# Two chained feed-forward layers behind chunked attention: each chunk attends to its own 64 slots, and the weights are normalised on VectorE

## The chip, the core and the metric

The kernel runs on one core of a Trainium2 chip. The metric is the device time of one execution in microseconds (us). The core has five engines that run their own instruction lists in order: TensorE (PE in the profile, with its weight loads as PEld), VectorE (DVE), ScalarE (ACT), GpSimd (POOL) and SyncE (SP, which issues the transfers here).

## What is computed

Attention over chunks of 32 tokens, then two feed-forward layers over all 3072 tokens (4 sequences of 768, 8 heads of 64, model width 512, hidden width 2048), all in 32-bit floats.

```python
chunk, left_ctx, right_ctx = (32, 16, 8)
for c in range(nc):                                   # 24 chunks of each of 4 sequences
    l_start = max(0, c_start - left_ctx)
    r_end = min(S, c_end + right_ctx)
    k_full = np.concatenate([mem_k, k[:, :, l_start:r_end]], axis=2)    # 8 memory slots + 56
    scores = scale * np.matmul(q_c, k_full.transpose(0, 1, 3, 2))
    scores = scores - np.max(scores, axis=-1, keepdims=True)
    a = np.exp(scores)
    a = a / (np.sum(a, axis=-1, keepdims=True) + 1e-09)
    out[:, :, c_start:c_end] = np.matmul(a, v_full)
h = x @ w_in;   g = np.maximum(0.01 * h, h);              x = g @ w_out      # first layer
h = x @ w_in2;  g = h * np.clip(h + 3.0, 0.0, 6.0) / 6.0; x = g @ w_out2     # second layer
```

A chunk in the middle of a sequence has exactly 64 slots: 8 memory slots, 16 tokens to its left, its own 32, and 8 to its right.

## The kernel before

**The feed-forward layers.** Tokens are taken in 6 blocks of 512, the hidden width in 16 slices of 128 (`f`). Per layer, block and slice PE runs 12 matmuls of 128x512 into `ph` (`hidden`) and 12 into `py` (`output`), since each 32-bit operand is split in a high and a low part and three of the four products are kept (`mm3`, L609). That is 4608 matmuls. Between the two, ACT and DVE apply the activation and split it again into `gh` and `gl` (L642, L651). The weights arrive as 64-bit words; converting one slice takes ACT (L219, L225, L253) and DVE (L229, L233, L240, L247, L259) five DVE instructions. The first layer's 32 half-slices are converted at the start and during its block 0, the second layer's during block 5.

**The attention.** Its unit is a pair of neighbouring chunks, 64 tokens: 48 pairs, 8 per block. A pair's 64 queries are multiplied with the 96 slots that the two chunks have together (`a_scores`, L346: 8 matmuls of 64x96, 16 records in the trace). Slots that a chunk may not see are barred, either by a matmul that adds minus infinity first (L337, 13 of the first 16 pairs) or by a mask that DVE adds (`a_masked`, L356). Then DVE takes the maxima (L376, L382), ACT the exponentials and their sums (L422), POOL adds a tiny number to the sums (L433), DVE inverts them (L437), and POOL multiplies the weights `e` by the inverse sums (`a_norm`, L441). The weights are turned, on PE and ACT for the first 16 pairs (`a_turn_pe` L459, `a_turned` L464), on DVE for the others (`a_turn`, L451), and multiplied with the values (`a_values`, L472: 8 matmuls of 64x64, 16 records). ACT and DVE split the result into the parts `xh` and `xl` of the layer's input (L488, L494).

**Where it is done.** The 8 pairs of block 0 come first, before any feed-forward matmul; the gaps on PE there are filled with warm-up matmuls on zeros (`keep_warm`, L701). A later pair is served by a visit: PE leaves the feed-forward matmuls, does the scores of one pair and the values of the pair before, and goes back. From the 17th pair on a visit serves two pairs ("doubled"): scores of two, values of two.

**What sets the order.** The program is written as steps with an engine, a length out of the table `TIME` and a due time. A planner (`Program.order`) runs through them ahead of time, gives each engine the ready step that is due first, fills PE's idle time before the last turning of block 0 with warm-up matmuls, and writes the instructions down in that order. Each engine then keeps it. `BEGIN`, `STEP_FIRST` and the like set due times; `SHIFTED` names pairs whose exponentials ACT takes in one instruction, for more work on DVE.

## Time and profile before

| | |
|---|---|
| device time, median of 3 runs | 1135.75 us (1135.74 to 1136.39) |
| device time of the profiled execution | 1135.49 us |
| its span, first to last instruction | 1133.7 us |
| PE busy | 1124.3 us, 99% of the span |
| PEld busy | 922.2 us, 81% |
| DVE busy | 589.5 us, 52% |
| ACT busy | 464.3 us, 41% |
| POOL busy | 60.9 us, 5% |

The times that follow are those of the profiled execution, counted from its span's start. [...]

### The profile page before, as it was taken

How to read it: one execution, taken by the hardware profiler on the slowest of the kernel's cores; microseconds unless marked ns; L12 is line 12 of the kernel's file. 1: busy time of each engine (PE TensorE's matmuls, PEld its weight loads, DVE VectorE, ACT ScalarE, POOL GpSimd, SP SyncE). 2: the span in 40 equal slices, each digit the busy share in tenths (PEclk: the TensorE clock that was granted, in tenths of full speed). 3: DMA queues.
4: the chain of work that ended last, by engine and by line, in shares of the span. 5: the costliest groups of instructions: out<-in, count | busy, mean ns of one | idle time of the engine just before them, and what ended most of it. 6: DMA issues, size and time to landing. Idle time of an engine off the chain costs nothing.

```text
span 1133.7 us, 16067 instructions
## 1 busy us (share of the span) xinstructions
PE 1124.3 (99%) x6326; PEld 922.2 (81%) x6326; DVE 589.5 (52%) x1280; ACT 464.3 (41%) x1043; POOL 60.9 (5%) x123
## 2 busy tenths in 40 slices
PE   8999999999999999999999999999999999999998
PEld 6787788888888888888888888888888888888887
DVE  6999955465665556656998623223223223222222
ACT  7988733334333343336777423223223223222222
POOL 4111100001000001000000000000000000000000
PEclk9999999999999999999999999999999999999999
DMA  8566421121111112115445102002002001001000
GB/s 261 182 187 188 144 75 38 38 85 65 38 56 57 51 62 75 38 64 184 151 150 178 63 1 75 1 1 75 1 1 75 1 1 38 1 1 38 1 1 37
DMA packets 31660, 78.63 MB, mean 69 GB/s; under 512 B 3424, under 2 KB 3424, under 8 KB 31584
## 3 DMA queue, kind: packets, MB, share of 16 engines
q1 hardware_dynamic: 31584, 77.61, 20.9%
q8 instruction: 49, 0.80, 0.3%
q14 instruction: 27, 0.22, 0.1%
HBM read 65.01 MB, written 12.58 MB: 68 GB/s over the span
## 4 chain that ended last, share of the span: by engine, by line
PE 95%; DVE 3%; ACT 1%; POOL 0%; issue 0%; POOLq 0%
PE ph L609 45%; PE py L609 45%; PE px L472 2%; PE psc L346 1%; DVE wa L240 1%; DVE w L259 0%; DVE wa L229 0%; DVE wa L233 0%; DVE raw L247 0%; ACT e L422 0%; PE warm L701 0%; PE pt L459 0%; DVE mx L376 0%; POOL e L441 0%; PE psc L472 0%
## 5 line engine op out<-in xcount | busy, mean ns | idle before, releaser
L609 PE MATMUL ph<-xh,w 128*128 128x512 f32 x768 | 254.3, 392 | 0.3 <-ACT xh L488 0.2
L609 PE MATMUL ph<-yh,w 128*128 128x512 f32 x768 | 252.0, 389 | 0.0
L609 PE MATMUL py<-gh,w 128*128 128x512 f32 x768 | 239.3, 392 | 0.8 <-DVE w L259 0.8
L609 PE MATMUL py<-w,gh 128*128 128x512 f32 x768 | 236.4, 389 | 0.0
L637 DVE SCALAR_TENSOR_TENSOR ph<-g,ph 128x512 f32<-128x512 f32 x96 | 66.8, 696 | 294.2 <-ACT g L631 294.2
L631 ACT ACTIVATE g<-ph,three 128x512 f32<-128x512 f32 x96 | 66.2, 690 | 299.8 <-PE ph L609 299.8
L609 PEld LDWEIGHTS ph<-xh,w 128*128 128x128 f32 x768 | 143.8, 188 | 31.6 <-DVE w L259 0.7
L609 PEld LDWEIGHTS py<-w,gh 128*128 128x128 f32 x768 | 144.1, 188 | 29.8
L609 PEld LDWEIGHTS ph<-yh,w 128*128 128x128 f32 x768 | 144.0, 188 | 29.9
L609 PEld LDWEIGHTS py<-gh,w 128*128 128x128 f32 x768 | 142.7, 188 | 31.3 <-DVE w L259 1.5
L609 PE MATMUL ph<-xl,w 128*128 128x512 f32 x384 | 149.6, 390 | 0.4 <-DVE xl L494 0.4
L609 PE MATMUL py<-gl,w 128*128 128x512 f32 x384 | 149.6, 390 | 0.0
L609 PE MATMUL py<-w,gl 128*128 128x512 f32 x384 | 149.4, 389 | 0.0
L609 PE MATMUL ph<-yl,w 128*128 128x512 f32 x384 | 149.4, 389 | 0.0
L628 ACT ACTIVATE ph<-ph 128x512 f32<-128x512 f32 x96 | 55.9, 582 | 177.9 <-PE ph L609 177.5
L451 DVE STREAM_TRANSPOSE aT<-e 32x128 f32<-32x128 f32 x384 | 116.0, 302 | 17.5 <-POOL e L441 12.0
L651 DVE TENSOR_TENSOR gl<-ph,gh 128x512 fp32r<-128x512 f32 x96 | 66.3, 690 | 74.1 <-ACT gh L642 73.1
L653 DVE SCALAR_TENSOR_TENSOR gl<-ph,gh 128x512 fp32r<-128x512 f32 x96 | 66.3, 691 | 55.6 <-ACT gh L644 55.6
L609 PEld LDWEIGHTS ph<-xl,w 128*128 128x128 f32 x384 | 72.1, 188 | 15.3 <-DVE xl L494 0.7
L609 PEld LDWEIGHTS py<-gl,w 128*128 128x128 f32 x384 | 72.1, 188 | 15.2
L609 PEld LDWEIGHTS py<-w,gl 128*128 128x128 f32 x384 | 72.1, 188 | 15.2
L609 PEld LDWEIGHTS ph<-yl,w 128*128 128x128 f32 x384 | 72.1, 188 | 15.0
(75 smaller groups left out, 910.0 us busy)
## 6 DMA issues: line engine op xcount, KB each, us to landing
raw<-in_moe_w_in_dram SPq DMA_DIRECT2D x32, 512.0 KB, 3.5
raw<-in_moe_w_out_dram SPq DMA_DIRECT2D x32, 512.0 KB, 3.7
qk_now<-in_qk_dram SPq DMA_DIRECT2D x24, 320.0 KB, 3.8
y_dram<-yo SPq DMA_DIRECT2D x24, 256.0 KB, 2.0
yn<-y_dram SPq DMA_DIRECT2D x6, 1024.0 KB, 6.0
out_dram<-oo SPq DMA_DIRECT2D x24, 256.0 KB, 3.3
in_qk<-in_qk_dram SPq DMA_DIRECT2D x16, 320.0 KB, 4.3
v_now<-in_v_dram SPq DMA_DIRECT2D x24, 192.0 KB, 2.5
```

The costliest lines, as they stand in the source:

```text
L240: nc.vector.scalar_tensor_tensor(out=a, in0=hi, scalar=0xC0000000, in1=a, op0=ALU.bitwise_and, op1=ALU.bitwise_or)
L346: nc.tensor.matmul(pt[j][n * PT:(n + 1) * PT, m * W:(m + 1) * W], qt[r, hp, :], kt[r, hp, :], start=not more, stop=True, tile_position=(e ...
L451: nc.vector.transpose(out=t[c, :, r], in_=e[r, :, c])
L472: nc.tensor.matmul(pt[e * D:(e + 1) * D, at + hp * every:at + hp * every + PT], vt[:, c], t[:, hp, n * PT:(n + 1) * PT], start=True, stop= ...
L609: nc.tensor.matmul(dst, a, b, start=first and i == 0, stop=last and i == len(terms) - 1)
L628: nc.scalar.activation(out=ph, in_=ph, func=AF.Prelu, alpha=0.01)
L631: nc.scalar.activation(out=g, in_=ph, func=AF.Relu, bias=three, scale=1.0)
L637: nc.vector.scalar_tensor_tensor(out=ph, in0=g, scalar=6.0, in1=ph, op0=ALU.min, op1=ALU.mult)
L651: nc.vector.tensor_sub(out=gl, in0=ph, in1=gh.bitcast(F32))
L653: nc.vector.scalar_tensor_tensor(out=gl, in0=ph, scalar=1.0 / 6.0, in1=gh.bitcast(F32), op0=ALU.mult, op1=ALU.subtract)
```

## The change

1. **Slots.** The two chunks of a pair no longer share 96 slots. The host lays out 104 slots for a pair (the 8 memory slots stand at both ends), the first chunk takes the first 64 of them and the second the last 64. Scores are 16 matmuls of 32x64 for a pair in place of 8 of 64x96, each into its own eighth of the array (64 rows by 32 columns). Nothing has to be barred in the middle of a sequence; only the first and last pair of each sequence overwrite a few scores. The barring matmuls, the mask and their memsets go.
2. **What follows from it.** `e` has 256 columns for a pair in place of 384. PE turns it with 2 matmuls in place of 4; DVE with 16 transposes of 32x64 in place of 12 of 32x128. Values are 16 matmuls of 64x32 in place of 8 of 64x64, on four places of 64x64 in place of two of 96x64, and land in two PSUM banks, in the free half of the banks of the visit's scores. So `xh` and `xl` take two instructions each in place of one.
3. **Normalising.** `a_norm` is issued on DVE in place of POOL.
4. **Transfers.** A pair's queries and keys are 344 KB in place of 328, its values 262 KB in place of 197 (128x672 and 128x512 words of 4 bytes, before 128x640 and 96x512).
5. **Order.** `TIME`, `BEGIN`, `STEP_FIRST`, `PAIR_FIRST`, `SHIFTED` (one pair in place of two) and `EARLY` have other numbers, so the planner writes another order. Before the first feed-forward matmul it has 59 pairs of warm-up matmuls (118 records) in place of 46 (92), and the first weights are loaded after the inputs of four pairs in place of one.

```diff
-    visit=1.45, visit2=2.1, scores=0.75, masked=0.56, most=0.55, exp=0.37, exp_all=0.52, small=0.15, inverse=0.18, norm=0.83, turn=0.6, turned=0.57, turn4=0.95,
-    values=0.85, xh=0.4, xl=0.45, half=1.36, act=0.58, six=0.69, gh=0.6, gl=0.69, done=0.66, warm=0.22,
+    visit=1.05, visit2=1.55, scores=0.5, masked=0.5, most=0.42, exp=0.35, exp_all=0.4, small=0.15, inverse=0.18, norm=0.36,
+    turn=0.35, turned=0.38, turn4=0.95, values=0.6, xh=0.52, xl=0.45, half=1.36, act=0.58, six=0.69, gh=0.6, gl=0.69,
+    done=0.66, warm=0.22,
...
-BEGIN = 31.0
-STEP_FIRST, STEP_MIXED, STEP = 7.0, 6.6, 5.5
-PAIR_FIRST = 1.9
-SHIFTED = (3, 5)
-EARLY = 35.0
+BEGIN = 34.0
+STEP_FIRST, STEP_MIXED, STEP = 6.6, 6.6, 5.5
+PAIR_FIRST = 2.1
+SHIFTED = (6,)
+EARLY = 30
...
-        more = barred_by_pe(pr)
-        if more:
-            for j in range(2):
-                nc.tensor.matmul(
-                    pt[j][:, :HP // 2 * W], cls, barred.rearrange("p m w -> p (m w)"),
-                    start=True, stop=False, skip_group_check=True,
-                )
-        for m in range(HP // 2):
-            for j in range(2):
-                hp = j * HP // 2 + m
-                for e in range(2):
-                    r, n = slice(e * D, (e + 1) * D), e ^ j
+        pt = [scores_of(pr, b) for b in range(2)]
+        for h in range(2):
+            for g in range(4):
+                c, n = divmod(g, 2)
+                for b in range(2):
+                    r = slice(b * D, (b + 1) * D)
                     nc.tensor.matmul(
-                        pt[j][n * PT:(n + 1) * PT, m * W:(m + 1) * W], qt[r, hp, :], kt[r, hp, :],
-                        start=not more, stop=True, tile_position=(e * D, n * PT), skip_group_check=more,
+                        pt[b][g * CH:(g + 1) * CH, h, :], qt[r, 2 * c + h, n * CH:(n + 1) * CH],
+                        kt[r, 2 * c + h, n * (W - WIN):n * (W - WIN) + WIN],
+                        start=True, stop=True, tile_position=(b * D, g * CH),
                     )
...
     def a_norm(pr):
-        e, su = e_t[pr], s_t.pop(pr)
-        nc.gpsimd.tensor_tensor(out=e, in0=e, in1=su.unsqueeze(2).to_broadcast([P, HP, W]), op=ALU.mult)
+        e, su = e_t[pr].rearrange("p h b w -> p (h b) w"), s_t.pop(pr)
+        nc.vector.tensor_tensor(out=e, in0=e, in1=su.unsqueeze(2).to_broadcast([P, HP, WIN]), op=ALU.mult)
...
-        for j in range(W // 32):
-            c = slice(32 * j, 32 * j + 32)
-            nc.vector.transpose(out=t[c, :, r], in_=e[r, :, c])
+        for b in range(2):
+            for j in range(WIN // 32):
+                c = b * WIN + 32 * j
+                nc.vector.transpose(out=t[c:c + 32, :, r], in_=e[r, :, b, 32 * j:32 * j + 32])
...
-        for hp in range(HP):
-            nc.tensor.transpose(pt[:W, hp * P:(hp + 1) * P], e[:, hp, :], ident)
+        for h in range(2):
+            nc.tensor.transpose(pt[:, h * P:(h + 1) * P], e[:, h].rearrange("p b w -> p (b w)"), ident)
...
-        for hp in range(HP):
-            for e in range(2):
-                c, n = slice(hp * P + e * D, hp * P + (e + 1) * D), e ^ 2 * hp // HP
-                nc.tensor.matmul(
-                    pt[e * D:(e + 1) * D, at + hp * every:at + hp * every + PT], vt[:, c], t[:, hp, n * PT:(n + 1) * PT],
-                    start=True, stop=True, tile_position=(0, e * D),
-                )
+        for n in range(2):
+            for h in range(2):
+                for b in range(2):
+                    for c in range(2):
+                        o = ((n * 2 + h) * 2 + c) * D
+                        g = 2 * c + n
+                        nc.tensor.matmul(
+                            pt[b][c * D:(c + 1) * D, h, n * CH:(n + 1) * CH], vt[b * WIN:(b + 1) * WIN, o:o + D],
+                            t[b * WIN:(b + 1) * WIN, h, g * CH:(g + 1) * CH],
+                            start=True, stop=True, tile_position=(b * D, c * D),
+                        )
...
-        c = add("POOL", T["norm"], due(4.6), a_norm, pr, after=[c])
+        c = add("DVE", T["norm"], due(4.6), a_norm, pr, after=[c])
```

**A doubled visit on PE**, in block 1. The names: `psc` holds scores, `qk_now` and `in_qk` are two pairs' queries and keys, `aT` turned weights, `v_now` and `in_v` values, `ph` is a feed-forward result. Before, its last scores and all its values:

```order
L346 MATMUL psc_0_2165<-in_qk 64x96 x2
L346 MATMUL psc_1_2166<-in_qk 64x96 x2
L472 MATMUL px_2183<-aT_2068,v_now 64x64 x8
L472 MATMUL px_2183<-aT_2083,in_v 64x64 x8
L609 MATMUL ph_1_7_2158<-xh_758,w_7_1075 128x512
```

Now, its last two scores and the beginning of its values:

```order
L349 MATMUL psc_0_2226<-in_qk 32x64
L349 MATMUL psc_1_2227<-in_qk 32x64
L472 MATMUL psc_0_2226<-aT_2092,v_now 64x32 x2
L472 MATMUL psc_1_2227<-aT_2092,v_now 64x32 x2
```

The visit stands where it stood, between the same kinds of feed-forward matmuls; in it are 32 score matmuls in place of 16 and 32 value matmuls in place of 16.

**DVE at the end of the start**, up to the last `xl` of block 0's eighth pair. `wa`, `raw` and `w` with the numbers of a slice and of its half are steps of the weight conversion (L229, L233, L240, L247, L259 in this order for each half-slice). Before:

```order
L259 TENSOR_TENSOR w_0_438<-raw_0_1_160,w_0_438 128x512
L229 TENSOR_SCALAR wa_2_0_563<-wa_2_0_563 128x512
L233 TENSOR_SCALAR wa_2_0_563<-wa_2_0_563 128x512
L240 SCALAR_TENSOR_TENSOR wa_2_0_563<-raw_2_0_221,wa_2_0_563 128x512
L494 TENSOR_TENSOR xl_286<-px_567,xh_285 128x4x64
L247 ISA raw_2_0_221<-raw_2_0_221,wa_2_0_563 128x512x2
L229 TENSOR_SCALAR wa_1_1_590<-wa_1_1_590 128x512
L233 TENSOR_SCALAR wa_1_1_590<-wa_1_1_590 128x512
L240 SCALAR_TENSOR_TENSOR wa_1_1_590<-raw_1_1_463,wa_1_1_590 128x512
L494 TENSOR_TENSOR xl_286<-px_603,xh_285 128x4x64
```

Now:

```order
L229 TENSOR_SCALAR wa_0_1_663<-wa_0_1_663 128x512
L233 TENSOR_SCALAR wa_0_1_663<-wa_0_1_663 128x512
L259 TENSOR_TENSOR w_1_675<-raw_1_0_188,w_1_675 128x512
L499 TENSOR_TENSOR xl_293<-px_0_678,xh_292 128x2x64
L499 TENSOR_TENSOR xl_293<-px_1_679,xh_292 128x2x64
L240 SCALAR_TENSOR_TENSOR wa_0_1_663<-raw_0_1_239,wa_0_1_663 128x512
L378 TENSOR_REDUCE mx_748<-psc_0_707 128x2
L378 TENSOR_REDUCE mx_748<-psc_1_708 128x2
L247 ISA raw_0_1_239<-raw_0_1_239,wa_0_1_663 128x512x2
L229 TENSOR_SCALAR wa_2_0_726<-wa_2_0_726 128x512
L499 TENSOR_TENSOR xl_293<-px_0_729,xh_292 128x2x64
L499 TENSOR_TENSOR xl_293<-px_1_730,xh_292 128x2x64
```

When the last `xl` is issued, 22 conversion instructions stand ahead of it on DVE before (half-slices 0_0, 1_0, 0_1 whole, 2_0 but for its last, three of 1_1) and 15 now (0_0 and 1_0 whole, 0_1 but for its last, one of 2_0). Up to the conversion's 29th half-slice, the order of both holds the same 29 on DVE, with 16 normalisations among them now.

## Rows read from the trace of the kernel before

**Rows 1.** Page, busy times: us, share of the span, instructions.

```profile
PE 1124.3 (99%) x6326; PEld 922.2 (81%) x6326; DVE 589.5 (52%) x1280; ACT 464.3 (41%) x1043; POOL 60.9 (5%) x123
```

**Rows 2.** Stretches (from:to, length), core 0: each engine's busy us, PEclk, DMA share, GB/s.

```profile
0.00:34.20 34.20, 29.37 (x413) 22.00 (x413) 24.90 (x71) 25.66 (x82) 13.86 (x37) 1.00 0.81 248
34.20:126.02 91.82, 91.00 (x598) 71.64 (x598) 88.22 (x177) 78.91 (x184) 14.06 (x22) 1.00 0.59 185
130.80:505.00 374.20, 374.20 (x2470) 307.92 (x2471) 215.83 (x612) 134.84 (x409) 32.98 (x64) 1.00 0.18 59
```

**Rows 3.** Chain that ended last, whole span: start us, us, engine, tile, line, records.

```profile
141.91 8.16 PE ph L609 x36
...
237.48 8.16 PE ph L609 x36
```

**Rows 4.** Chain that ended last, 140 to 220 us: a doubled visit.

```profile
155.51 0.82 PE psc L346 x32
156.33 1.08 PE px L472 x32
157.41 2.95 PE py L609 x12
160.36 2.72 PE ph L609 x12
```

**Rows 5.** Chain that ended last, 100 to 145 us: a single visit, conversion, turning.

```profile
115.15 0.18 PE psc L337 x2
115.33 0.49 PE psc L346 x16
115.82 0.61 PE psc L472 x16
...
124.75 1.28 DVE w L259
...
127.49 0.44 PE pt L459 x4
```

**Rows 6.** Stretches inside a visit, L346 on PE alone: records under way.

```profile
155.46:155.56 0.10, 0.10 (x4) 1.00 0.00 0
155.58:155.64 0.06, 0.06 (x8) 1.00 0.00 0
155.66:155.72 0.06, 0.06 (x12) 1.00 0.00 0
```

**Rows 7.** Timeline of POOL, 37 to 40 us: start us, us, instruction, idle before it.

```profile
37.86 1.12 POOL L441 TENSOR_TENSOR e<-e,su 128x384 f32<-128x384 f32 x1 [0.36 <-DVE su L437]
```

**Rows 8.** Timeline of DVE, 0 to 60 us.

```profile
31.28 0.42 DVE L494 TENSOR_TENSOR xl<-px,xh 128x256 fp32r<-128x256 f32 x1
31.62 0.68 DVE L247 CUSTOM_DVE_ANT_0 raw<-raw,wa 128x1024 uint16<-128x1024 uint16 x1
...
38.21 1.32 DVE L247 CUSTOM_DVE_ANT_0 raw<-raw,wa 128x1024 uint16<-128x1024 uint16 x1
...
41.68 0.69 DVE L247 CUSTOM_DVE_ANT_0 raw<-raw,wa 128x1024 uint16<-128x1024 uint16 x1
```

**Rows 9.** Groups by line and shape: xcount, busy us, mean ns, idle before.

```profile
L356 DVE SCALAR_TENSOR_TENSOR e<-psc,masks 128x192 f32<-128x192 f32 x70 | 20.5, 349 | 36.3 <-PE psc L346 36.2
L382 DVE TENSOR_REDUCE mx<-e 128x4 f32<-128x384 f32 x35 | 17.8, 543 | 0.0
...
L376 DVE TENSOR_REDUCE mx<-psc 128x2 f32<-128x192 f32 x26 | 8.0, 347 | 0.8 <-PE psc L346 0.8
...
L494 DVE TENSOR_TENSOR xl<-px,xh 128x256 fp32r<-128x256 f32 x9 | 3.7, 407 | 0.0
```

**Rows 10.** Timeline of PE, the start: warm-up, the feed-forward's second matmul.

```profile
13.21 1.04 PE L701 MATMUL warm<-idle 128*128 128x256 bf16 x8
...
34.21 0.50 PE L609 MATMUL ph<-xl,w 128*128 128x512 f32 x1 [0.38 <-DVE xl L494]
```

More of the change, by code (lines that the diff above doesn't have):

```diff
@@ L487, in a_xh @@
         c = slice((i - 1) * PT if doubled(pr) else i * PT, (i + 1) * PT)
-        nc.scalar.copy(out=x_t[0, blk][0][:, :, c], in_=px_t[pr])
+        for b in range(2):
+            nc.scalar.copy(out=x_t[0, blk][0][:, 2 * b:2 * b + 2, c], in_=px_t[pr][b])
     def a_xl(pr):
@@ L557, in attention @@
         if direct:
-            c = add("DVE", T["most"] + 0.06, due(1.2), a_most, pr, after=[c])
+            c = add("DVE", T["most"], due(1.2), a_most, pr, after=[c])
             c = add("POOL", T["small"], due(1.8), a_scaled, pr, after=[c])
             if pr in SHIFTED:
-                c = add("DVE", T["masked"] + 0.06, due(2.0), a_shift, pr, after=[c], takes=e, frees=s)
+                c = add("DVE", T["masked"], due(2.0), a_shift, pr, after=[c], takes=e, frees=s)
                 c = add("ACT", T["exp_all"], due(2.6), a_exp_all, pr, after=[c])
@@ L568, in attention @@
         else:
-            c = add("DVE", T["masked"] + 0.06, due(1.1), a_masked, pr, after=[c] + set_up, takes=e, frees=s)
+            c = add("DVE", T["masked"], due(1.1), a_edge, pr, after=[c] + set_up, takes=e, frees=s)
             c = add("DVE", T["most"], due(1.7), a_most, pr, after=[c])
@@ L587, in attention @@
         if blk == 0:
[L588 removed]
+            p = [("ph", ("v", pr, b)) for b in range(2)]
             c = add("PE", T["values"], due(7.0), a_values_first, pr, after=[c, vl], takes=p, frees=aT + vv)
@@ L597, in visit_step @@
             return add("PE", T["scores"], t, visit, pr, after=[*after, opened[-1]], takes=takes, frees=frees)
-        p = [("ph", ("x", pr))] if doubled(pr) else takes[-1:]
+        p = takes or [(f"pa{j}", ("s", pr, j)) for j in range(2)]
         c = add("PE", T["visit2"] if doubled(pr) else T["visit"], t, visit, pr,
-                after=[x for q in pending for x in q[:2]] + [*after], takes=[*takes] + (p if doubled(pr) else []),
+                after=[x for q in pending for x in q[:2]] + [*after], takes=p,
                 frees=[k for q in pending for k in q[2]] + [*frees])
```

185 lines of the change are left out of this document (86 added, 99 removed).

## The prediction

> **What bounds the kernel now.** I read the page first: PE is busy for 1124.3 of 1133.7 us [rows 1], and the stretch 130.8 to 505 us has no idle on it [rows 2]. So from there on an instruction off PE costs nothing unless PE comes to wait for it, and a microsecond taken from PE's list is a microsecond of the end. Next, the chain of waits: in block 1 it is PE alone. Twelve feed-forward matmuls take 2.72 us. A doubled visit is 0.82 us of scores and 1.08 us of values, and the twelve matmuls behind it take 2.95, that is 0.23 more [rows 4]: **2.13 us a visit**. The check is the distance of two blocks, 237.48 - 141.91 = 95.57 us [rows 3]: 32 times 2.72 are 87.04, and four visits at 2.13 are 8.52.
>
> The time ahead of that has two parts. Until 34.2 us PE is busy 29.4 us, much of it warm-up, and the feed-forward starts when the last of block 0's attention is there: its second matmul waits for `xl` [rows 2, 10]. From 34.2 to 126 us PE is full, but so nearly is DVE, 88.2 of 91.8 us, ACT less with 78.9 [rows 2]: weights are converted just ahead of their use, and at 124.75 the chain leaves PE for a conversion's last step [rows 5]. PE and DVE bound that part together. DVE has 24.9 + 88.2 = 113.1 us of work up to 126 us and 12.9 us idle, 9.3 of them in the start.
>
> **The doubled visits.** The order holds 16 visits with scores of two pairs, 15 with values of two, one with values of one, and one last with values alone: 32 pairs' scores and 33 pairs' values. First the old price in parts. A record of the turning takes 0.44 / 4 = 110 ns for 128 columns [rows 5], 0.86 ns a column, one at a time. A score record of 96 columns would take 82 ns alone. They follow each other by 0.82 / 32 = 25.6 ns, so 3.2 run beside each other on the four places they use. The stretches show how: between 155.46 and 155.56 four are under way and none starts, then eight, then twelve [rows 6]; they start in groups of four, a group each 82 ns. A value record of 64 columns would take 55 ns, and they follow by 1.08 / 32 = 33.8: 1.6 on two places. Both come to 80% of the places.
>
> Now there are 64 score records of 64 columns, 55 ns alone, on eight places. At 80% of eight, 6.4, they follow by 8.6 ns: 64 of them take 0.55 us. If no more than 3.2 run at a time, which is the most a row shows, they take 1.10. I take 0.55, since the share of places was the same on two and on four. The 64 value records have 32 columns, 27.5 ns alone, on four places: at 3.2 they follow by 8.6 ns, again 0.55 us. But each still loads weights of 64 columns, and no row shows a place taking such weights more often than each 55 ns; at that pace 64 x 55 / 3.2 = 1.10 us, as now. Between 0.55 and 1.10 no row is nearer, so I take 0.8. With 0.23 for leaving and coming back a visit is 1.58 us. That is 16 x 0.27 for scores and 16.5 x 0.28 for values: **8.9 us less**. The bounds are 1.33 us a visit (13 less) and 2.43 us (4.9 more).
>
> [...] No row here shows a 64-column load under a shorter matmul.
>
> **What DVE pays for the normalising.** 48 of them move from POOL; 16 lie before 126 us. A DVE instruction over 256 columns has a mean of 407 ns, and the next starts 0.34 us after it (31.28 to 31.62) [rows 8, 9]: I take 0.38, 16 x 0.38 = 6.1 us more. Against it stands what POOL's multiplication does to DVE now. At 37.86 it runs on POOL for 1.12 us; the DVE instruction issued at 38.21 takes 1.32 us, where the same one takes 0.69 at 41.68 [rows 7, 8]. This stands at all eight multiplications between 34.2 and 126 us, up to the 1.28 us at 124.75 [rows 5], with 0.5 to 0.6 us more each, 4.6 together; in the start I count 1.1. With POOL's instruction gone these go: 5.7 less.
>
> The other DVE instructions up to there, by the difference of 192 and 384 columns, 347 and 543 ns [rows 9], some 1 ns a column: 26 maxima of 128 for 192 columns, -1.8; ten mask and shift instructions of 192 become eight of 128, two at 20.5 / 70 = 0.29 and eight by 0.07, -1.1; five reductions of 384 become four of 256, one at 17.8 / 35 = 0.51 and four by 0.13, -1.0; 15 `xl` become 30 halves, 15 more starts at 0.07 (the 0.34 us less 256 columns at 1 ns), +1.0. The sum is 6.1 - 5.7 - 1.8 - 1.1 - 1.0 + 1.0 = **2.5 us less work on DVE**, to the same 29th half-slice. After 130.8 us DVE has 216 of 374 us of work [rows 2]; 32 normalisations there add 12 and are hidden, as are 16 transposes of half the columns in place of 12.
>
> **The start.** PE's list there gains 26 warm-up records at 1.04 / 8 = 0.13 us [rows 10], +3.4. It loses eight barrings of 0.18, -1.4; half of eight turnings of 0.44, -1.8; and on nine pairs' scores of 0.49 and eight pairs' values of 0.61 [rows 5], at the ratios above (0.55 of 0.82, 0.8 of 1.08), -1.5 and -1.3. That is 2.6 less, and the feed-forward starts at 31.6 if PE's waits stay as they are. If scores and values gain nothing there, 34.4; if the waits shrink with the chain's shorter steps, 29. The transfers don't stop it: queries and keys of the eighth pair have the same 5.4 MB up to and with them, as weights now stand behind more of the inputs. The later weights are what the start pays with: 7 conversion instructions fewer are done when the feed-forward starts, 3.9 us by the conversion's five steps of some 0.35 to 0.69 us. DVE's work in the start is then 24.9 - 3.9 - 0.7 (mask memsets), the other changes there cancelling within 0.5: 20.3 us. Idle is 31.6 - 20.3 = 11.3 in place of 9.3.
>
> So up to the 29th half-slice DVE has 2.5 + 0.7 = 3.2 us less work and 2.0 us more idle: 1.2 us earlier. PE would be through sooner (it saves visits and turnings here too), so what it saves in block 0 is not counted. Behind 34.2 us DVE had 3.6 us idle while PE was as full as itself; with PE waiting for DVE some of it goes, from none to half. I take a quarter, 0.9: **2.1 us earlier**. The bounds: a start of 34.4 us has 14.1 idle, 4.8 more, and gives 1.6 later; a start of 29 has 0.6 less, and with half of the 3.6 gives 5.6 earlier.
>
> **The sum.** 8.9 + 2.1 = 11.0 us off a device time of 1135.49 us for the profiled execution (span 1133.7, 1.8 us around it) is 1124.5. The median of the runs is 0.26 us above that execution: 1124.7.
>
> **Rivals.** (a) Slower: small matmuls have a floor. The shortest mean distance of records is 25.6 ns, that of the scores. If that is what an instruction costs PE and not the sharing of places, 128 records take 3.28 us a visit: +0.82 on scores and +0.56 on values, 16 x 0.82 + 16.5 x 0.56 = 22.4 us more, 1158 with the start as it was. It turns against the change from 1.90 us / 128 = 14.8 ns a record. Against it: records start in fours with a pause of a record's length between [rows 6], so four are issued in less than a third of that length, and the pause follows the columns.
> [...]
> (b) Slower: neither eight places nor shorter value records help, 2.43 us a visit: +4.9, -2.1 in block 0, 1138.5. Nothing in the trace runs on eight places, so nothing excludes it.
> (c) Faster by less: one of the two helps and the other doesn't (1.88 us a visit, 4.1 less), or DVE holds block 0 up (1.6 later in place of 2.1 earlier): 1128.5 to 1133.
> (d) Faster by more: both at their best, 13 off in the visits, and 5.6 off in block 0: 1117.
>
> **How the numbers follow.** Forecast, 1120 to 1128.5: 0.57. (c), 1128.5 to 1133: 0.17. (d), under 1120: 0.11, a third of that under 1116. (b): 0.07, and (a): 0.08. The range 1116 to 1133 leaves out (a), (b) and the tail of (d), 0.19. A measurement of this kernel can tell about 0.2% from no change, 2.3 us. Faster by more: 0.57 + 0.17 + 0.11 = 0.85. Of (b), between its cases, 0.03 lies within 2.3 us and 0.04 above: same 0.03, slower 0.12.
>
> **What would show it.** In the changed profile a doubled visit's scores should be one piece of the chain of 64 records in 0.5 to 0.6 us, its values 64 records in 0.55 to 1.1, and two blocks 93 to 94 us apart. DVE instructions of 1.0 to 1.3 us in block 0 should be gone, with the normalisation near 0.4 us. The first feed-forward matmul should come at 29 to 34 us, and between it and 125 us PE should wait for conversions where it is full now. I am wrong if the visit comes to 2 us or more, if `gl` comes late behind normalisations and transposes so that PE waits in blocks 1 to 4, or if block 0 ends later than now.

## The result, and the profile after

The changed kernel takes **1142.53 us** (median of 4 runs, 1141.01 to 1144.28) against 1135.74 for the kernel before beside it: a ratio of 1.0057 [1.0045, 1.0069], slower by 0.57% where 0.97% faster (1124.7 us) was forecast. The profiled execution took 1143.07 us, its span is 1141.3 us, 7.6 us above that of before.

Busy times of the changed kernel, as in [rows 1]: PE's hardly moved, though it has 1504 records more.

```profile
PE 1124.9 (99%) x7830; PEld 920.2 (81%) x7830; DVE 590.1 (52%) x1453; ACT 455.6 (40%) x1082; POOL 26.4 (2%) x94
```

The same three stretches as in [rows 2] (from:to, length, then the engines' busy us with records, PEclk, DMA share, GB/s), changed kernel:

```profile
0.00:34.20 34.20, 29.15 (x678) 21.51 (x678) 19.32 (x68) 20.95 (x90) 4.71 (x21) 0.95 0.64 232
34.20:126.02 91.82, 87.13 (x787) 67.32 (x783) 86.51 (x191) 75.12 (x183) 6.43 (x13) 0.98 0.58 197
130.80:505.00 374.20, 372.14 (x3508) 305.26 (x3508) 216.92 (x744) 130.56 (x427) 13.96 (x59) 1.00 0.21 68
```

In the start DVE does 19.3 us of work where it did 24.9. From 34.2 to 126 us PE, which was as good as full (0.8 us idle), is idle for 4.7 us, and behind 130.8 us, where it had no idle at all, it has 2.1. Of the 4.7 us the larger part is put down to ACT, to the step L253 of the weight conversion: four waits of 0.7 to 0.8 us. The page of the changed kernel, then of before, first group of feed-forward matmuls (whole run; behind the last bar the idle time ahead, and what ended most of it):

```profile
L616 PE MATMUL ph<-xh,w 128*128 128x512 f32 x768 | 259.3, 396 | 7.5 <-ACT w L253 3.1
```

```profile
L609 PE MATMUL ph<-xh,w 128*128 128x512 f32 x768 | 254.3, 392 | 0.3 <-ACT xh L488 0.2
```

So DVE isn't the only engine that PE waits for in block 0. No run alters ACT's order alone.

Where the 7.6 us arise is read best from the feed-forward matmuls, which are the same 4608 in both kernels. This table is worked out from their starts in the traces: the start before, and by how much each kernel is later (+) at the same matmul, when both are counted from their first matmul of all (at 1.04 us of the span, at 1.17 in the kernels with the wider warm-up of `w_512`). The second matmul stands at the opening of block 0, and 349 near its end; 433 lies in block 1; at 769, 1153 and 1537 the blocks 2, 3 and 4 begin.

```
matmul  before   after n_pool b_norm b_turns s_early s_old  w_512   c_1    c_3    c_5
     2   34.21   +1.91  +1.27  -1.04   +1.27   +4.26  +2.77  -1.06  +1.74  +1.95  +2.48
    97   59.85   +2.53  +1.86  -1.05   +2.82   +3.29  +3.25  -0.61  +0.77  +1.11  +2.84
   349  130.69   +4.90  +3.16  +0.42   +5.29   +3.74  +3.40  +1.79  +1.27  -0.83  +1.04
   433  149.90   +5.22  +3.59  +0.42   +7.22   +4.07  +5.95  +2.12  +3.19  +1.09  +2.96
   769  234.59   +5.09  +3.45  +0.42   +5.14   +3.94  +3.73  +1.99  +1.08  -1.02  +0.85
   865  258.49   +5.99  +4.19  +0.70   +5.13   +4.84  +4.61  +2.89  +1.06  -1.03  +0.81
  1153  330.17   +5.89  +4.09  +0.70   +5.03   +4.74  +4.51  +2.79  +0.94  -1.15  +0.69
  1249  354.06   +6.83  +4.99  +0.99   +5.39   +5.69  +5.47  +3.94  +1.31  -0.75  +0.65
  1537  425.74   +6.73  +4.88  +0.99   +5.29   +5.59  +5.37  +3.84  +1.19  -0.87  +0.53
  1633  449.63   +7.68  +5.78  +1.27   +5.65   +6.54  +6.33  +5.60  +1.58  -0.51  +0.52
  4608 1129.55   +7.60  +5.70  +1.27   +5.57   +6.46  +6.26  +5.52  +1.48  -0.60  +0.43
```

For the changed kernel that is +4.9 in the start and block 0, +0.3 at the beginning of block 1 (not followed up), +2.8 in three steps of 0.9 where blocks 2, 3 and 4 begin, and -0.4 over the visits, which were to give 8.9. The visit, the block's end and the start each have their own cause. (In row 433 a jump of some 2 us that is gone in row 769, as in `b_turns`, says only that one visit stands ahead of that matmul there and behind it before.)

**The visit.** Timeline of PE, changed kernel, the visit that answers to [rows 4] (start us, us, instruction; a group's us run from its first start to its last end; the ends of matmuls are modelled by the profile, so paces are read from starts):

```profile
160.65 0.46 PE L349 MATMUL psc<-qk_now 64*32 64x64 f32 x32
160.92 0.59 PE L349 MATMUL psc<-in_qk 64*32 64x64 f32 x32
161.44 0.67 PE L472 MATMUL psc<-aT,v_now 64*64 64x32 f32 x32
161.93 0.65 PE L472 MATMUL psc<-aT,in_v 64*64 64x32 f32 x32
```

From the first score to the first value it is 0.79 us (before 0.82), from there to the matmul at 162.50 it is 1.06 (before 1.08), and by the starts around it the way out and back costs 0.25 (before 0.23): 2.10 us in place of 2.13, the same in nearly all visits. The last record of a group of scores lasts 0.216 us, so the first 32 start within 0.46 - 0.22 = 0.24 us, 7.7 ns apart. The second 32 start within 0.59 - 0.22 = 0.37 us, 12 ns apart. Then nothing starts for 0.15 us, and the values follow by (0.67 - 0.22) / 31 = 14.6 ns, on four places, so that a place takes one each 58 ns.

**A block's end.** Timeline of DVE, changed kernel, where block 1 ends, then PE's of the same time (in brackets the idle time ahead and what ended it):

```profile
241.56 0.69 DVE L658 TENSOR_TENSOR gl<-ph,gh 128x512 fp32r<-128x512 f32 x1
242.17 0.68 DVE L689 COPY yo<-py 128x512 f32<-128x512 f32 x1
242.88 4.98 DVE L447 STREAM_TRANSPOSE aT<-e 32x64 f32<-32x64 f32 x20
247.89 0.69 DVE L658 TENSOR_TENSOR gl<-ph,gh 128x512 fp32r<-128x512 f32 x1
```

```profile
248.64 0.50 PE L616 MATMUL ph<-xh,w 128*128 128x512 f32 x1 [0.64 <-DVE gl L658]
```

Between two `gl` stand a copy and 20 transposes in one piece, so the second `gl` comes 247.89 - 241.56 = 6.33 us behind the first. PE needs 2 x 2.72 = 5.44 us for the two groups of twelve matmuls that it runs meanwhile, 0.89 less, and it waits: the next matmul into `ph` is released by that `gl`. The 0.89 us are the step in the table. Before, with 12 transposes there, the two `gl` stood 5.11 us apart, and PE didn't wait:

```profile
236.66 0.69 DVE L651 TENSOR_TENSOR gl<-ph,gh 128x512 fp32r<-128x512 f32 x1
237.26 0.68 DVE L682 COPY yo<-py 128x512 f32<-128x512 f32 x1
237.98 3.77 DVE L451 STREAM_TRANSPOSE aT<-e 32x128 f32<-32x128 f32 x12
241.77 0.69 DVE L651 TENSOR_TENSOR gl<-ph,gh 128x512 fp32r<-128x512 f32 x1
```

**The start.** Timeline of PE, changed kernel:

```profile
17.41 0.41 PE L349 MATMUL psc<-in 64*32 64x64 f32 x21
20.12 0.45 PE L349 MATMUL psc<-in 64*32 64x64 f32 x11 [2.30 <-issue]
20.51 2.85 PE L708 MATMUL warm<-idle 128*128 128x256 bf16 x14
```

In the middle of one pair's scores PE stops for 2.30 us, and nothing that the profile shows ("issue") ended it. Behind it 14 warm-up matmuls take 2.85 us, 0.20 us each where it was 1.04 / 8 = 0.13 before [rows 10]. The stretches show the clock, and how full the transfers were:

```profile
15.00:18.00 3.00, 2.82 (x97) 1.86 (x94) 2.29 (x7) 2.33 (x12) 0.33 (x1) 1.00 1.05 393
18.00:21.00 3.00, 0.88 (x14) 0.58 (x15) 0.37 (x2) 0.69 (x4) 0.23 (x1) 0.75 1.00 393
21.00:24.00 3.00, 3.00 (x66) 2.09 (x65) 1.77 (x7) 1.29 (x8) 0.52 (x1) 0.68 0.16 57
36.00:39.00 3.00, 3.00 (x9) 2.40 (x9) 2.68 (x7) 3.00 (x11) 0.23 (x1) 0.59 0.65 217
```

The granted clock is 1.00 until 19.49 us, 1.67 us after PE came to stand, then 0.50 until 22.90 us, and DVE and ACT have next to nothing to do from 18 to 21 us. It is 0.50 a second time from 36.56 to 39.96 us, behind PE's wait of 1.48 us for `xl` ahead of the first feed-forward matmul (36 to 39 us: 0.59). That a stop brings the clock down isn't shown: in `n_pool` the clock is 1.00 from 18 to 30 us, around a stop of 2.54 us. The kernel before had no stop for "issue" in its start, and its clock stands at 1.00 in all these stretches. Up to the end of the 29th half-slice, one stretch of each kernel (changed, then before; DVE is the third engine):

```profile
0.00:131.43 131.43, 120.90 (x1479) 91.95 (x1479) 110.86 (x269) 100.86 (x287) 12.46 (x35) 0.97 0.59 204
```

```profile
0.00:126.01 126.01, 120.37 (x1011) 93.64 (x1011) 113.11 (x247) 104.56 (x266) 27.91 (x59) 1.00 0.65 202
```

DVE's work fell by 2.3 us, its idle time rose from 12.9 to 20.6.

### The profile page after: what moved, and what is told of

It is laid out like the page before. It is cut to its first block, busy times and chain, and to the rows that moved or that the text cites. A ratio compares the mean times of both kernels' runs of the same rounds, so it can differ in the third digit from the quotient of the medians.

```text
span 1141.3 us, 19214 instructions
## 1 busy us (share of the span) xinstructions
PE 1124.9 (99%) x7830; PEld 920.2 (81%) x7830; DVE 590.1 (52%) x1453; ACT 455.6 (40%) x1082; POOL 26.4 (2%) x94
## 4 chain that ended last, share of the span: by engine, by line
PE 87%; DVE 7%; ACT 3%; issue 1%; POOL 0%; ACTq 0%; POOLq 0%; DVEq 0%
PE py L616 41%; PE ph L616 41%; DVE aT L447 2%; PE psc L472 2%; PE psc L349 1%; ACT e L416 1%; PE warm L708 1%; DVE wa L240 1%; DVE w L259 1%; DVE raw L247 1%; DVE gl L658 1%; ACT w L253 0%; ACT gh L649 0%; ACT wa L219 0%; DVE wa L233 0%
## 5 line engine op out<-in xcount | busy, mean ns | idle before, releaser
L616 PE MATMUL ph<-xh,w 128*128 128x512 f32 x768 | 259.3, 396 | 7.5 <-ACT w L253 3.1
L447 DVE STREAM_TRANSPOSE aT<-e 32x64 f32<-32x64 f32 x512 | 120.9, 236 | 7.4
```

Of the source, the lines that this page charges most:

```text
L447: nc.vector.transpose(out=t[c:c + 32, :, r], in_=e[r, :, b, 32 * j:32 * j + 32])
L616: nc.tensor.matmul(dst, a, b, start=first and i == 0, stop=last and i == len(terms) - 1)
```

## The experiments

Each kernel differs from the changed one by the diff shown ("..." marks what is left out of it), but for `b_norm`, which starts from the kernel before. The changed kernel took 1142.53 us; the kernel before, beside the others, 1135.9 to 1136.1 us.

### Which half of the change costs the time

`n_pool`: chunks keep their own slots, POOL multiplies.

```diff
-        nc.vector.tensor_tensor(out=e, in0=e, in1=su.unsqueeze(2).to_broadcast([P, HP, WIN]), op=ALU.mult)
+        nc.gpsimd.tensor_tensor(out=e, in0=e, in1=su.unsqueeze(2).to_broadcast([P, HP, WIN]), op=ALU.mult)
...
-        c = add("DVE", T["norm"], due(4.6), a_norm, pr, after=[c])
+        c = add("POOL", T["norm"] + 0.3, due(4.6), a_norm, pr, after=[c])
```

> The changed kernel with the multiplication by the inverse sums back on POOL (planned with 0.66 us there); chunks keep their own 64 slots. Theory: the engine of this step is not what costs the time. Block 0 loses 16 times 0.43 us of DVE and gets holds of DVE by POOL back, of 0.3 to 0.6 us each: within 1.5 us of 1142.5. Rival: normalising on VectorE lengthens what stands ahead of `gl` and of the conversions and is the cause of the loss: 1136 to 1139 us.

Measured: 1141.94 us, ratio to before 1.0054 [1.0037, 1.0071]. The theory holds: with slots of their own, the engine of this step isn't what costs the time. DVE is through with the 29th half-slice at 129.69 us, 1.7 us sooner than in the changed kernel:

```profile
0.00:129.69 129.69, 121.21 (x1489) 92.18 (x1489) 107.32 (x254) 100.08 (x287) 21.84 (x51) 0.99 0.61 207
```

That is 3.5 us less work than with the multiplication on DVE, holds included, and 1.8 us more idle. The 0.6 us between the medians is inside the scatter of the runs.

`b_norm`: the same two lines in the kernel before, the other way round (`nc.vector`, `"DVE"`, `T["norm"] - 0.3`).

> The kernel before with the other half of the change alone: the weights are multiplied by their inverse sums on VectorE (planned with 0.53 us), 96 slots for a pair as before. Theory: the move costs and gives about the same in block 0 (16 times 0.53 us of DVE for 384 columns, 8.5 us, against holds of 5.7 us) and is hidden later: 1136 to 1139 us. Rival: it is the half of the change that costs the time: 1141 us or more.

Measured: 1138.79 us (1136.75 to 1140.34), ratio 1.0023 [1.0014, 1.0033]. So this half alone costs 2.8 us, inside the expected range, and the other half alone (`n_pool`) 5.9; together 6.8. Of the 2.8 the profiled execution, the shortest of its ten, shows 0.4 in block 0 and three steps of 0.28 at the block ends. In it DVE is through with the 29th half-slice at 126.43 us, 0.4 us later than before:

```profile
0.00:126.43 126.43, 120.50 (x1017) 94.26 (x1017) 116.05 (x263) 103.48 (x265) 10.93 (x43) 1.00 0.64 201
```

That is 2.9 us more work on DVE and 2.5 us less idle, and PE, which waits for that step in both kernels, is later by the same 0.4 us.

### The visit

`v_swap`: the scores of the second pair first.

```diff
-            a_scores(pr)
             if doubled(pr):
                 a_scores(pr + 1)
+            a_scores(pr)
...
```

(Left out: whichever pair comes first now takes the two banks.)

> The changed kernel with the two pairs' scores of a doubled visit in the other order: the 32 records on `in_qk` first, then the 32 on `qk_now`. In the changed kernel the first 32 (on `qk_now`) start within 0.24 us, the second 32 take 0.38 us and more. Theory: PE holds only so many instructions ready, and those beyond arrive at a slower pace; so whichever pair stands second is the slow one, here `qk_now`. Rival: the operand `in_qk`, which lies in a buffer of the raw weights, is what is slow: then the first 32 are spread now, and the second 32 start within 0.24 us. The time is that of the changed kernel, 1142.5 us, by both.

Measured: 1140.92 us, one run. Timeline of PE:

```profile
181.05 0.45 PE L349 MATMUL psc<-in_qk 64*32 64x64 f32 x32
181.31 0.59 PE L349 MATMUL psc<-qk_now 64*32 64x64 f32 x32
```

The second 32 are the slow ones again, now those on `qk_now`: it isn't the operand `in_qk` that is slow.

`v_32`: values with 32 weight columns, first halves ahead of second halves, in doubled visits.

```diff
-                            start=True, stop=True, tile_position=(b * D, c * D),
...
+        k = 32 if doubled(pr) else D
+        for d in range(0, D, k):
...
+                            r = c * D + d
...
+                                start=True, stop=True, tile_position=(b * D, r),
```

> The changed kernel with each value matmul of a doubled visit cut in two of 32 weight columns, all first halves ahead of all second halves: 128 records in place of 64, each on a place of 64x32, on four places at a time. In the changed kernel a place takes a value record each 58 ns, with 32 columns moving as with the 64 of before. Theory: it is the load of 64 weight columns that takes those 58 ns. Then 32 columns take about half, 128 records follow by some 7.3 ns, values take 0.93 us in place of 1.06 and a visit 1.95 in place of 2.08: 2 us less in 16 visits, 1140.5 us. Rival: a place takes 58 ns for a record whatever its columns: 128 records take 1.86 us, a visit 2.9 us, 1155 us.

Measured: 1149.96 us, ratio 1.0120 [1.0105, 1.0136]. The time misses both, yet the visit answers the question. Timeline of PE, an undisturbed visit, its larger groups:

```profile
211.30 0.54 PE L349 MATMUL psc<-in_qk 64*32 64x64 f32 x28
211.61 0.21 PE L475 MATMUL psc<-aT,v_now 64*32 64x32 f32 x1
...
211.68 0.71 PE L475 MATMUL psc<-aT,v_now 64*32 64x32 f32 x60
...
212.22 0.75 PE L475 MATMUL psc<-aT,in_v 64*32 64x32 f32 x62
```

60 records start within 0.71 - 0.19 = 0.52 us, 8.8 ns apart; on four places that is one each 35 ns, where 64 weight columns took 58. So a place isn't held 58 ns whatever its columns; that it is the load of the weights which takes them, and not what else hangs on their number, is the likely reading. Two more things are seen. Values start at 211.61, before the last scores have started: the pause of 0.15 us between scores and values is gone here, where both use places of 64x32. And behind the first 32 scores the records come by some 9 ns on the mean, scores or values, so the 35 ns may be that pace and the load shorter. With twice the records at this pace the undisturbed visit still takes 2.10 us, where the theory had 1.95. The 7.4 us lost against the changed kernel lie elsewhere. With 192 records a visit PE stops inside visits, too:

```profile
162.98 0.60 PE L475 MATMUL psc<-aT,in_v 64*32 64x32 f32 x44
165.53 0.37 PE L475 MATMUL psc<-aT,in_v 64*32 64x32 f32 x18 [1.95 <-issue]
```

and the waits at the block ends grew with it.

`v_first`: values ahead of both pairs' scores. The function `visit` in short:

```diff
-        a_scores(pr); a_scores(pr + 1)
         for i, p in enumerate(of):
             a_values(p, [x[:, :, i * PT:(i + 1) * PT] for x in px])
+        a_scores(pr); a_scores(pr + 1)
```

> The changed kernel with the values of a visit ahead of its scores; nothing else differs, the planner's list is the same. Theory: behind the first 32 records PE's instructions come by some 8.3 ns a record (with the values in 128 records, they followed by 16.6 ns for two), so the second 32 score records were spread. A place takes a value record each 58 ns, four places one in 14.6 ns, slower than instructions come, so some are ready again when the scores begin. Expected: 64 values in 1.0 us, then 64 scores without the spread, 0.5 to 0.6 in place of 0.79 us, a visit of 1.85 to 1.95 in place of 2.08 us, 2 to 3 us less in 16 visits: 1139.5 to 1140.5 us. Rival: the second pair's scores are slow for being the second 32 on the same places: a visit stays at 2.08 us and the time at 1142.5 us.

Measured: 1142.55 us (1140.70 to 1145.60). The visit is what it was, 1.06 and 0.79 us, with 32 scores starting within 0.24 and 32 within 0.38 us again. The expected gain wasn't there. That left two readings: more than 32 records without a pause, or the second use of the same places.

`v_mid`: values between the two pairs' scores, edited likewise.

> The changed kernel with the values of a visit between the scores of its two pairs. The second 32 score records were spread whichever pair they belong to and whatever stands ahead of the first 32. Theory: some 32 records are ready ahead of PE, later ones come by 8.3 ns; the values take 14.6 ns a record, so 32 are ready again behind them. Expected: both pairs' scores start within 0.24 us each; one more change between scores and values costs 0.15 us, so a visit stays near 2.08 us. Rival: the second use of the same places is what is slow: the second pair's records are spread over 0.37 us again, and a visit takes 2.2 us. Time 1141 to 1145 us by both.

Measured: 1141.28 us, one run. Timeline of PE:

```profile
181.41 0.45 PE L347 MATMUL psc<-qk_now 64*32 64x64 f32 x32
181.79 0.67 PE L470 MATMUL psc<-aT,v_now 64*64 64x32 f32 x32
182.28 0.65 PE L470 MATMUL psc<-aT,in_v 64*64 64x32 f32 x32
182.85 0.46 PE L347 MATMUL psc<-in_qk 64*32 64x64 f32 x32
```

Both pairs' scores go within 0.24 us now, on the same places. So it is the second 32 of 64 in a row that are slow (0.37 us), and not the second use of the places (0.24); the visit is no shorter (2.08 us), as the 0.14 us gained pay one more pause of 0.15.

### The start

`w_512`: each pair of warm-up matmuls in one (the zeros have 512 columns).

```diff
-    idle = at.tile([P, 256], BF, tag="idle", name="idle")
+    idle = at.tile([P, 512], BF, tag="idle", name="idle")
...
-        for c in range(2):
-            r = slice(c * 256, c * 256 + 256)
-            nc.tensor.matmul(late["warm"][:, r], idle[:, :P], idle, start=True, stop=True)
+        nc.tensor.matmul(late["warm"], idle[:, :P], idle, start=True, stop=True)
```

> The changed kernel with each pair of warm-up matmuls of 256 columns written as one of 512: the same time on PE by the columns, 59 instructions with their 59 weight loads less in the start. In the changed kernel PE stops for 2.30 us at 17.82 us, in the middle of a pair's scores, after 347 of its records; in other variants of it PE stopped 2.2 to 2.5 us at the 221st or the 347th record, at whatever place of the program that was, and each time 2.4 to 2.6 us behind the start of a 16 KB transfer of PE's own instructions. Theory: PE runs out of instructions, as their transfer stands behind the inputs' transfers. Expected: with 31 records less up to that place the stop goes or moves to another place of the program, again at about the 221st or 347th record; if it goes, the 2.30 us and the slow clock behind it (1.2 us) are off the start, and the time is 1139 to 1140 us. Rival: PE waits there for a pair's inputs: it stops in the same scores as before, 1142.5 us.

Measured: **1140.28 us** (1138.87 to 1141.19), ratio 1.0037 [1.0024, 1.0049], 2.2 us less than the changed kernel. The stop stands one pair's scores later in the program, with 20 of 32 still to come, and lasts 0.86 us in place of 2.30:

```profile
19.21 0.33 PE L349 MATMUL psc<-in 64*32 64x64 f32 x12
20.40 0.41 PE L349 MATMUL psc<-in 64*32 64x64 f32 x20 [0.86 <-issue]
```

The stretches up to the long stop, of the changed kernel, `v_first`, `n_pool`, `s_old` and `w_512`, point to the cause; the first number in brackets is PE's records until then.

```profile
0.00:20.10 20.10, 15.58 (x347) 10.85 (x347) 7.79 (x30) 11.15 (x53) 2.83 (x15) 0.98 0.93 340
```

```profile
0.00:19.10 19.10, 15.44 (x347) 10.70 (x347) 7.74 (x30) 11.17 (x53) 2.85 (x15) 1.00 0.93 340
```

```profile
0.00:19.65 19.65, 15.08 (x346) 10.80 (x347) 6.12 (x26) 11.01 (x52) 5.00 (x18) 1.00 0.93 337
```

```profile
0.00:21.60 21.60, 16.10 (x346) 11.54 (x347) 10.77 (x39) 12.13 (x50) 3.17 (x14) 1.00 0.91 337
```

```profile
0.00:20.35 20.35, 17.28 (x346) 8.10 (x346) 9.81 (x37) 12.53 (x61) 3.35 (x16) 1.00 0.92 338
```

In all five PE stands after 346 or 347 records, at different places of the program (the first two have the same start). The stop ahead of it stands after 220 or 221: 0.54 us in the changed kernel, 1.83 in `s_old`, 2.38 in `s_early`. Between the two lie 126 matmuls with as many weight loads. In the changed kernel a 16 KB transfer of instructions starts 2.52 and 2.60 us ahead of the two stops' ends (at 11.43 and 17.52 us), and the transfers ran at 378 and 397 GB/s meanwhile. The reading: PE has used up what it holds before the next 16 KB are there. Its rival, that PE waits there for a pair's inputs, doesn't fit a stop that moves through the program with the count of records. That these transfers are PE's follows from their number in the whole run, 61 for 15660 matmuls and loads and 49 before for 12652, one for each 257 or 258; between the two stops lie 252 of them. The queue of these transfers in the first 34.2 us (number, MB, share of 16 engines), changed kernel, then before:

```profile
q8 instruction: 5, 0.08, 0.9%
```

```profile
q8 instruction: 3, 0.05, 0.6%
```

The kernel before had used 286 records up to 23.1 us, the changed one 347 before 18.

`s_early`: weights' transfers earlier (`EARLY` 38 in place of 30).

> The changed kernel with `EARLY` at 38 in place of 30: the first weights are loaded behind the inputs of one pair, as before the change, and 21 conversion instructions stand ahead of the start's last `xl` on DVE in place of 15. Theory: DVE's idle of the start, some 8 us more than before the change, comes from the weights' late transfers and is what block 0 ends later by. Expected: six instructions of about 0.6 us done earlier, so 3 to 4 us less idle on DVE up to the first feed-forward matmul, that matmul still at about 35.8 us, block 0's last conversion 3 to 4 us earlier, 1139 us. Rival: the transfers are full in the start, so inputs of later pairs come later by the weights put ahead of them (three times 0.5 MB at some 390 GB/s, 4 us): the first feed-forward matmul moves to 38 to 40 us, and the time stays at 1142.5 us or grows.

Measured: 1141.44 us (1139.73 to 1141.92), ratio 1.0044 [1.0029, 1.0059]. Both happen. The first feed-forward matmul is 2.3 us later than in the changed kernel, as the rival had it, with the stop at the 221st record 2.38 us long; and with six conversion instructions more behind it, block 0 ends 1.2 us earlier in the profiled execution. The 1.1 us between the medians lies within the overlap of the runs.

`s_old`: the planner's dates of before.

```diff
-BEGIN = 34.0
-STEP_FIRST, STEP_MIXED, STEP = 6.6, 6.6, 5.5
-PAIR_FIRST = 2.1
-SHIFTED = (6,)
-EARLY = 30
+BEGIN = 31.0
+STEP_FIRST, STEP_MIXED, STEP = 7.0, 6.6, 5.5
+PAIR_FIRST = 1.9
+SHIFTED = (3, 5)
+EARLY = 35.0
...
-            attention(pr, block_at[0, blk] - (6 if blk == 1 else 6) - every * (NPB - i), blk == 1, 1.6 if blk == 1 else 3.4)
+            attention(pr, block_at[0, blk] - (4.5 if blk == 1 else 6) - every * (NPB - i), blk == 1, 1.6 if blk == 1 else 3.4)
```

> The changed kernel with the planner's dates of before: `BEGIN` 31, `STEP_FIRST` 7.0, `PAIR_FIRST` 1.9, `SHIFTED` (3, 5), `EARLY` 35 and 4.5 for block 1's pairs; 18 conversion instructions stand ahead of the start's last `xl` in place of 15. Theory: the start's loss comes from PE (warm-up written between the pairs, and the stop for instructions), so the dates alone give back little: 1140 to 1143 us. Rival: the new dates are what costs DVE its idle: block 0 ends where it did before the change, some 5 us earlier, 1137 us.

Measured: 1141.98 us (1139.70 to 1142.49), ratio 1.0049 [1.0034, 1.0064]: the theory's. It has the stops of 1.83 and 1.60 us, and the dates alone aren't the cause (1.5 of the 4.9 us at matmul 349 in the table).

### The block ends

`b_turns`:

```diff
-    turn=0.35, turned=0.38, turn4=0.95, values=0.6, ...
+    turn=0.35, turned=0.38, turn4=1.1, values=0.6, ...
```

> The changed kernel with one number of the planner's table altered: four transposes of DVE are planned with 1.1 us in place of 0.95. The planner then writes 16 of them between two `gl` at the end of blocks 1 to 4 where it wrote 20. Theory: 20 transposes and a `gl` take 4.98 + 0.69 = 5.67 us, PE needs 5.44 us for the two groups of twelve matmuls that run meanwhile, and it waits for the second `gl`; that is the 0.9 us by which each of these blocks is longer than before. Expected: the 0.9 us goes at the four block ends, 3.6 us together, 1139 in place of 1142.5 us. Rival: the transposes written behind the second `gl` make the visit's values late instead and PE waits there: no change, 1142.5 us.

Measured: **1140.47 us** (1137.15 to 1141.10), ratio 1.0032 [1.0021, 1.0043], 2.1 us less than the changed kernel. DVE at the end of block 1:

```profile
242.93 3.97 DVE L447 STREAM_TRANSPOSE aT<-e 32x64 f32<-32x64 f32 x16
246.94 0.69 DVE L658 TENSOR_TENSOR gl<-ph,gh 128x512 fp32r<-128x512 f32 x1
```

The second `gl` now comes 5.33 us behind the first, in place of 6.33, and PE doesn't wait. (The expectation got its 0.9 us from 5.67 against 5.44, which is 0.23; it left out the copy between the two `gl`.) In the table the step at block 2 is gone, those at blocks 3 and 4 are 0.36 in place of 0.95: 2.1 of the 2.8 us. (The expectation counted four ends; three have the step.)

### Together

`c_1` is `w_512`, `b_turns` and `s_early` in one.

> The changed kernel with the three edits together that each took some time off: warm-up in matmuls of 512 columns, the planned 1.1 us for four transposes, and `EARLY` at 38. Theory: the three act at different places (the stop of PE in the start, the block ends, the conversions ahead of the first feed-forward matmul), so their gains add: -2.2, -2.1 and -1.1, 1137 us, still above the kernel before. Rival: the earlier weights bring the stop for instructions back, as the transfers stand longer: 1139 to 1141 us.

Measured: 1137.05 us (1136.71 to 1138.55), ratio 1.0009 [1.0000, 1.0019]: the gains add, as expected (5.5 us of 6.8), and 1.1 us above the kernel before are left. `c_3` has the values ahead of scores as well, and this:

```diff
-        nc.vector.tensor_tensor(out=e, in0=e, in1=su.unsqueeze(2).to_broadcast([P, HP, WIN]), op=ALU.mult)
+        (nc.gpsimd if pr < 2 * NPB else nc.vector).tensor_tensor(out=e, in0=e, in1=su.unsqueeze(2).to_broadcast([P, HP, WIN]), op=ALU.mult)
...
-        c = add("DVE", T["norm"], due(4.6), a_norm, pr, after=[c])
+        c = add("POOL" if pr < 2 * NPB else "DVE", T["norm"] + 0.3 * (pr < 2 * NPB), due(4.6), a_norm, pr, after=[c])
```

> All of these together: warm-up of 512 columns, 1.1 us planned for four transposes, `EARLY` at 38, values ahead of scores in a visit, and the multiplication by the inverse sums on POOL for the first 16 pairs and on VectorE for the rest. Theory: 1137 by the first three, 2 to 3 us less by the visits, and 1 to 2 less as DVE's list of block 0 gets shorter (3.5 us less work up to the 29th half-slice with POOL multiplying, 2 us more idle): 1132 to 1134 us, less than either kernel. Rival: in block 0 the chain over POOL is longer and PE waits for it, and the visits' gain is not there: 1137 us or more.

Measured: 1134.90 us (1134.50 to 1137.22), ratio 0.9992 [0.9983, 1.0002]. Block 0 came out as expected, 2.1 us below `c_1`; the visits gave nothing, so it misses the expected 1132 to 1134 and stands level with the kernel before. `c_5` is `c_3` with 1.2 us planned for four transposes.

> As c_3 (warm-up of 512 columns, `EARLY` at 38, values ahead of scores, POOL multiplying for the first 16 pairs), with four transposes planned at 1.2 us in place of 1.1. In c_3 two of the four block ends still lose 0.3 us each, where 16 transposes stand before a `gl` and 16 behind it; with 1.2 the planner writes 12 there. Theory: these 0.6 us go, 1134.3 us, and the kernel is below both others by more than its spread. Rival: DVE's transposes then stand in the way later, at the visit's values: 1134.9 us or more.

Measured: **1134.28 us** (1133.73 to 1136.04) against 1136.12, ratio **0.9982 [0.9973, 0.9991]**: below both kernels, by 0.18% below the one before. The 0.6 us against `c_3` are those of the theory. Its profiled execution is the longest of its eleven runs, so its column starts high; what it shows is that no step is left at the block ends.

## Why the prediction was wrong

The profiled execution took 1143.07 us where the sum had 1124.5. Of these 18.6 us the visits are 8.5 (8.9 less forecast, 0.4 measured), the start and block 0 are 7.0 (2.1 earlier forecast, 4.9 later measured), the block ends 2.8, forecast at nothing, and the beginning of block 1 is 0.3. All three signs of being wrong that the prediction named came: the visit above 2 us, `gl` late, block 0 later.

**The visit's price, term by term.** The forecast had 0.55 for the scores, 0.8 for the values and 0.23 for the way out and back; measured 0.79, 1.06 and 0.25. This step failed by most. The reading of [rows 6] was right in its core: eight places do run beside each other, and 32 records start in 0.24 us. Three things were mis-sized. (1) The old 0.82 us was divided by 32 records, and the quotient scaled with the number of places. But some 0.15 us of it are pauses: in the trace of before the second group of four starts 0.05 us late, and from the last score to the first value it is 0.17 us where groups follow by 0.08. The pause at that change is still 0.15 us on the changed kernel's eight places. (2) The pace of the first 32 doesn't hold for 64: 0.24 us, then 0.37 (`v_swap`, `v_first`, `v_mid`). (3) The values' 0.8 was a middle between "scales" and "the weights' load sets the pace"; a place took a record each 58 ns with 64 weight columns and each 35 ns with 32 (`v_32`), of which not all need be the load, and the values came out near the upper bound. So the scores' 4.3 us of gain hung on a mean that mixed a pace with a pause, and the values' 4.6 us on the middle between two readings.

**Rival (a), the floor of 25.6 ns a record,** was wrong as well: records follow by 7.7 ns up to 32, and beyond by 12 in the changed kernel and some 9 in `v_32`. The visit's mean, (0.79 + 1.06) / 128 = 14.5 ns, is next to its turning point of 14.8 all the same, by the pause of 0.15 us, the slower second 32 and the values' 14.6 ns. Rival (b), 2.43 us a visit, is nearer to the 2.10 that came than the forecast's 1.58, but had block 0 end early.

**DVE's work** was right: 3.2 us less was forecast to the 29th half-slice, measured 2.3. The holds by POOL's multiplication are gone; the normalisation takes 425 ns where 0.38 us was assumed. Its 16 come to 6.8 us where 6.1 were forecast, against the 5.7 us of holds that POOL's multiplication cost before: 1.1 us more, in place of 0.4. Against the same slots with POOL multiplying (`n_pool`) the move costs 3.5 us, so the holds there come to 6.8 - 3.5 = 3.3 us, an estimate: POOL's multiplication over 256 columns cost DVE less than the one over 384.

**DVE's idle in the start** is the second step that failed: +2.0 us forecast, +7.7 measured to the 29th half-slice, 5.6 of them up to 34.2 us. "If PE's waits stay as they are" is the clause that broke. They didn't: 13 more warm-up pairs, and 16 records more for each pair's scores and as many for its values, stood ahead of two stops of 0.54 and 2.30 us, after 220 and 347 records, with the clock of 0.50 behind the second; by the reading under `w_512` PE used its instructions up faster than they came. The sum had no term for that. The feed-forward's second matmul, which stood at 34.2 before and was forecast at 31.6, came at 36.1 us, outside the 29 to 34.4 that bounded the sum. `w_512` takes 3.1 of the 4.9 us at the 349th matmul away and leaves 1.8; with earlier weights as well 1.3 are left (`c_1`), and with less DVE work in block 0 the kernel is 0.8 ahead of before there (`c_3`).

**"32 normalisations and 16 transposes are hidden"** is the third failed step. They are hidden by DVE's share of busy time (217 of 374 us), and not where it counts. 16 transposes of 64 columns take 4.0 us where 12 of 128 took 3.8, as half the columns cost 236 ns and the whole 302, while the planner, whose entry stayed at 0.95 us for four in place of three, put 20 of them between two `gl`. The prediction had named just this sign ("`gl` late behind normalisations and transposes") and given it no price: 2.8 us in three block ends.

**The range** stopped at 1133 on the slow side because the only slow cases in it were those of the visit. A slow start was bounded by PE's list alone.

What stays open: how the 4.9 us of the start divide between the stop, the clock and the weights, as each edit moves the others; how much of block 0 is ACT's; and what fills the 1.41 and 1.56 us from the end of an instruction transfer's record (12.54 and 18.56 us in the changed kernel) to PE's next instruction. The scatter of the changed kernel's runs (3.3 us, before 0.8) goes along with their granted clock: 1141.01 and 1141.98 us at 0.999, 1143.07 at 0.997, 1144.28 at 0.995. So does that of `b_norm`, 1136.75 to 1138.16 us at 0.999 and above and 1139.42 to 1140.34 at 0.998 and below, and the profiled execution is one of the former, which is why its median shows 1.5 us more. Why the clock falls in some executions and not in others stays open.

## What to carry to other kernels

Before a mean distance of records is scaled, split it into pace and pause (here some 0.15 of 0.82 us were pauses): look at the starts inside the group and at the gap to the next group. Count instructions as a resource of their own: smaller matmuls for the same work raised the matmuls and loads here from 12652 to 15660 and their 16 KB transfers from 49 to 61, and PE stopped for 0.54 and 2.30 us, in waits nobody had named, while the transfers ran at 378 and 397 GB/s. Work on an engine that is half idle (DVE, 52%) was not hidden where it stood in one piece, 20 transposes of 4.98 us, ahead of the one `gl` that PE waited for; the planner's table has to be measured again with every change of shape (1.1 in place of 0.95 us for four transposes took 2.1 us off).

## What the runs showed of the hardware

- 32 score records on eight places start in 0.24 us, 7.7 ns apart. Of 64 in a row the second 32 take 0.37 us; with 64 value records between them, 14.6 ns apart, both take 0.24 us (`v_mid`). What makes the second 32 slow was not shown.
- From scores on 64x32 places to values on 64x64 places, or back, PE started nothing for 0.15 us (changed kernel, `v_first`, `v_mid`); with the same shape there was no such pause (`v_32`).
- PE stopped for 0.23 to 2.54 us when it had done 218 to 221 or 342 to 347 matmuls, at one of the two places or both, in every kernel here whose chunks have their own slots, and in neither of the others. From the start of the 16 KB instruction transfer to the end of the stop it was 2.52 and 2.60 us in the changed kernel, and the transfers ran at 378 and 397 GB/s.
- A DVE transpose of 32x64 took 236 ns, with starts 0.25 us apart, and one of 32x128 302 ns, with starts 0.31 us apart.
